# Moving four key projections and one set of values from between the attention layers into them

## The chip, the cores and the metric

The kernel runs on one core of a Trainium2 chip. The core has five engines that run their own instruction queues in order and meet only through semaphores: TensorE (PE, matrix products into the accumulator memory PSUM, with its weight loads shown as PEld), VectorE (DVE), ScalarE (ACT), GpSimd (POOL) and SyncE (SP, which issues the DMA transfers). The metric is the device time of one execution in microseconds; lower is better.

## The reference

Four layers act on one sequence of S = 2048 rows of D = 512 numbers: a sliding-block layer (A), a full layer (B), and both again. Each normalises its rows, projects them to queries, keys and values of 32 heads of 16 numbers, takes a softmax of scaled scores, sums the values with it, projects the result and adds it to the rows. Cut to what matters:

```python
x = x + _A_ref(_layernorm(x), A_wqkv, A_wo)     # row i sees rows i-255 .. i
x = x + _B_ref(_layernorm(x), B_wqkv, B_wo)     # every row sees every row
x = x + _A_ref(_layernorm(x), A_wqkv, A_wo)
x = x + _B_ref(_layernorm(x), B_wqkv, B_wo)

# inside both:
q, k, v = split_heads(x @ wqkv)
p = softmax(mask(q @ k.T * 16 ** -0.5))          # the mask only in A
out = merge_heads(p @ v) @ wo
```

## The kernel before

**Numbers.** Activations and weights are split into a high and a low float16 part, and a product is the sum of three products of parts (`TERMS`). A projection of 512 rows to 512 columns is therefore four tiles of 128 columns, each twelve products (four blocks of the inner dimension, three terms). One such product is a *piece*; the planner counts it as `MM` = 0.222 us. Twelve pieces end up in one PSUM bank or bank pair, `b`. Values are also made in half widths (`halves`): a piece is then half as long.

**Layers and chunks.** Layers are numbered 0 to 3; 0 and 2 slide, 1 and 3 are full. The rows are cut into NQ = 4 chunks of 512 (`c`). Heads are handled four at a time (`qd`, 8 of them); a column tile `ht` (or `t`, 0 to 3) of a projection holds eight heads, so it serves two `qd`. In the full layers one pass over all keys for one chunk and one `qd` is a *visit* of NT = 16 steps. In each step, for two pairs of heads, PE makes scores (L764), ACT takes their exponential (`e`, L772, 128x1024 numbers at a time), and PE multiplies an earlier step's exponentials with the values (L821) into `acc`. Layer 1 goes chunk by chunk (visits 0 to 7 are chunk 0, 8 to 15 chunk 1, ...). Layer 3 goes column tile by column tile, in 16 groups of two visits.

**Side work.** Everything else, the projections for the same layer and for the next, norms, transposes and output projections, is cut into pieces and put between the attention's steps by a planner that runs when the kernel is built. It fixes the order of PE's instructions (and in the full layers DVE's) with a clock of its own, `clock[0]`. A `Work` is a generator with a cost, a name, the names that it depends on, and, with `w`, a weight tile that must have been loaded (it becomes ready 8 us of the planner's clock after the load; ring 0 has two such tiles). A `Side` holds a list of works for a stretch of steps. In a sliding layer `step` runs works up to a share of the whole cost. In a full layer it calls `share`, after the second scores of every step but a visit's first, with one more call in the visit's second step, so that a visit has sixteen calls. `share` adds to `budget` the cost still left divided by the steps still left (at least `least`), caps it at 0.75 us, and runs pieces of the first work in the list that is ready, until about two full pieces have run, the budget is used up, or `b` isn't free. After the twelfth piece `b` counts as taken for another 2 us (`PH["free"]`), while DVE joins its two halves, so that a call is lost there.

**Squares and shifts.** After a key or query projection the sums of squares of its rows are needed (`sq`, on ACT or POOL; summed on PE by `hsum`, L556 or L559). This last part (`rest`) is put on the list `pend`, due 4.6 us later in a full layer, and `settle` carries it out, in `share` only when `b` isn't in use; `b` then counts as taken for 2 us again. For queries it gives the row maxima `m`, which are written to `qs` (L603). For keys it gives maxima in `KM`, and with the last chunk of a column tile `key_shift` makes the tile's shift from all four chunks, writes it to `kf` (L624) and notes `("S", l, ht)` as done. The keys of a full layer lie in DRAM as `kf`, the queries as `qs`; `kt` and `qt` are the tiles loaded from them for a visit (L795, L786).

**When a visit may start.** `attention` loads `kt` and `qt` of the next visit as soon as neither `lacking` (the key and query projections that it needs) nor `owing` (their shift or maxima) holds. If a visit begins and that hasn't happened, it forces side work out:

```python
            if not win and not ahead:
                while lacking(c, qd) or owing(c, qd):
                    if lacking(c, qd) or PH["busy"]:
                        sd.one(True)
                    else:
                        settle()
                ahead.append(load_full(l, c, qd))
```

**Which work goes where.** Layer 0's works (`side0`) hold the key projections K(1,0), K(1,1) and K(1,2) of layer 1, four column tiles each, beside its own. Its tail (`tails[0]`), which runs without attention, ends with layer 1's transposes T(1,3) and the last chunk's keys for tiles 0 and 1 (K1(0), K1(1)). Layer 1 has two Sides: one for the first four visits, `works[1][0]`, which `finish` empties by force at its end, and one for the rest of the layer, `works[1][1]` (`side1()`), with 14 full projections. The tail of layer 2 (`tails[2]`) has values of layer 3 (VV(3,...)), the output projection OO(2,3), transposes T(3,3) and the keys K3(3,0). Layer 3's sixteen Sides come from `side3(t, c)`; at a group's end all but output projections (`O3`, which have no name) must be finished.

Of the kernel before, what the change touches and what calls it, by code (L numbers as in the profile page):

```python
# [35 lines left out]
RINGS = WB, VB  # L36
L_MIN = 2.0 ** -90
# [153 lines left out]
def fast_path(ctx, tc, flag, a_x, a_wqkv, a_wo, b_wqkv, b_wo, out):  # L191
# [298 lines left out]

    def project(l, s, c, act, ht=None, ring=0):


        ty, n = l % 2, f"{l}_{s}_{c}" + ("" if ht is None else f"_h{ht}")
        w = weights(ty, s, n, *((0, D, 0) if ht is None else (ht * P, (ht + 1) * P, ring)))
# [9 lines left out]
        for t in range(NHT) if ht is None else (ht,):  # L505
            ps = bank()
            w0 = t * P if ht is None else 0
# [54 lines left out]
    def quarters(ht):  # L562

        return slice(0, P) if ht is None else slice(32 * ht, 32 * ht + 32)

    def keys(l, c, act, ht=None, then=None, ring=0):
        sqs = yield from project(l, 1, c, act, ht, ring)

        def rest():
            ph = squares(f"k{l}_{c}_{ht}", sqs)  # L570
            if l not in KM:
                KM[l] = vp.tile([P, NQ], F32, name=f"km{l}", tag="km", bufs=2)
            r = quarters(ht)
            with tc.high_priority(HEAD_START):
                nc.vector.tensor_reduce(KM[l][r, c:c + 1], ph[r], axis=AX.XY if PH["full"] else AX.X, op=ALU.max)  # L575
                if then is not None:
                    then(l, ht)
        pend.append((clock[0] + (4.6 if PH["full"] else 3.6 if PH["win"] else 1.2), rest, (l, c, ht)))
# [347 lines left out]
    class Side:  # L926

        def __init__(self, steps, works=(), following=(), least=0.0):
            self.next, self.least = list(following), least
            self.q, self.steps, self.cost, self.spent, self.k = [], steps, 0.0, 0.0, 0  # L930
            self.budget = self.lag = 0.0
            for w in sorted(carried + list(works), key=lambda w: PH.get("full") and w.name is None):
                self.add(w)
            carried.clear()
# [56 lines left out]

        def share(self):

            self.budget = min(self.budget + max((self.cost - self.spent) / max(self.steps - 3 - self.k, 1), self.least), 0.75)
            self.lag = max(self.lag - 0.42, -0.3)
            if pend and not PH["busy"] and clock[0] >= max(PH["free"], pend[0][0], vt_[0] - 0.2):
                settle(False)
                PH["free"] = clock[0] + 2.0
                self.lag += 0.1
            s0 = self.spent  # L1000
            while (self.q and clock[0] >= PH["free"] and self.budget >= MM / 2 and (self.lag < 0.25 or self.budget > 0.45)
                   and self.spent - s0 < 1.5 * MM):
# [6 lines left out]
        def finish(self, keep=False):  # L1009

            stays = lambda w: (w.name is None and keep) if w.name is None else w.name[0] == "P"
# [17 lines left out]
    def attention(l, works):  # L1029
# [18 lines left out]
        for (g, c, qd), after in zip(visits, visits[1:]):  # L1048
# [27 lines left out]
            for f in (attn_win if win else attn_full)(l, c, qd, *ops, a):  # L1076
                drain()
                if f is None:
                    flush(1)
# [35 lines left out]
    def K(l, c, act=True):  # L1115
        return Work(later(keys, l, c, act), PK, ("K", l, c), [("T", l, c), ("P", l % 2, 1), ("P", l % 2, 0)], True)
# [12 lines left out]
    def K1(ht, act=False):  # L1129
        return Work(later(keys, 1, NQ - 1, act, ht, key_shift, act), PK / 4, ("K1", ht), [("T", 1, NQ - 1), ("P", 1, 1)], True, ring=act)  # L1130
# [108 lines left out]
    def side1():  # L1239
        m = [(ty, s) for ty in range(2) for s in range(4)]  # L1240
        a = [CW(*x, [("C", *y)] if y else [("Q", 1, 1)]) for y, x in zip([None] + m, m)]
        a += [Q(1, c, False) for c in (1, 2, 3)]
        for c in range(3):
            a += [OO(1, c), T(2, c)] + ([Q(2, c - 1, False)] if c else []) + [K(2, c, False), VV(2, c, False)]
        return a

    def side3(t, c):
# [6 lines left out]
        if t < 2 and (t or c > 1):  # L1254
            a.append(upper(3, 2 * t + c // 2, range(2 * (c % 2), 2 * (c % 2) + 2)))
        if (t, c) != (0, 0):
# [3 lines left out]
    works = [[side0(c) for c in range(NQ)], [[last_lower(1), K1(2), upper(1, 2), upper(1, 3), K1(3)], side1()], [side2(c) for c in range(NQ)],  # L1260
# [3 lines left out]
             2: [VV(3, 0, True, (0,)), OO(2, 3, True), VV(3, 1, True, (0,), late(3)), VV(3, 2, True, (0,), late(3)), VV(3, 0, True, (1,), late(3)), T(3, 3), K3(3, 0, True, True)]}  # L1264
# [54 lines left out]
```

## Time and profile before

| | us |
|---|---|
| median of three runs | 2701.3 |
| the runs | 2702.79, 2701.3, 2694.14 |
| profiled execution | 2691.39 |
| its span, first to last instruction | 2689.5 |
| first scores of layer 1 | 447.45 |
| first scores of layer 3 | 1706.87 |

In the span, PE is busy 92% and ACT 88%. The granted clock of TensorE averages 0.993 of full speed. Times in timelines are counted from the start of the span. A row of a timeline has the start, the time, the engine, the line, the operation, output and inputs with buffer numbers left out, and the number of instructions merged into the row; in brackets stands how long the engine was idle before it and what it waited for. A matmul's shown time contains its way through the array, some 0.2 us, in which the next one already runs, so merged rows of PE overlap by that much. In the chain of waits a row has its start, its time, and the engine and line, or the DMA, on which the end depended at that moment.

### The profile page before, as it was taken

How to read it: one execution, taken by the hardware profiler on the slowest of the kernel's cores; microseconds unless marked ns; L12 is line 12 of the kernel's file. 1: busy time of each engine (PE TensorE's matmuls, PEld its weight loads, DVE VectorE, ACT ScalarE, POOL GpSimd, SP SyncE). 2: the span in 40 equal slices, each digit the busy share in tenths (PEclk: the TensorE clock that was granted, in tenths of full speed). 3: DMA queues.
4: the chain of work that ended last, by engine and by line, in shares of the span. 5: the costliest groups of instructions: out<-in, count | busy, mean ns of one | idle time of the engine just before them, and what ended most of it. 6: DMA issues, size and time to landing. Idle time of an engine off the chain costs nothing.

```text
span 2689.5 us, 120844 instructions
## 1 busy us (share of the span) xinstructions
PE 2470.9 (92%) x54767; PEld 1135.1 (42%) x54767; DVE 1107.3 (41%) x2350; ACT 2363.7 (88%) x2671; POOL 529.4 (20%) x1072
## 2 busy tenths in 40 slices
PE   7889999999998999999999999899999999998996
PEld 3334454444443444444444444534444443433332
DVE  5576453223334334334336666233333333333333
ACT  4666765999999999999996776799999999999996
POOL 1556550001000100100116886000000000000000
PEclk9999999999999999999999999999999999999998
DMA  8898875232334325324227655423333323333332
GB/s 277 248 287 266 237 200 156 67 97 89 107 94 125 96 86 151 100 87 114 93 82 209 193 166 163 133 83 112 93 94 101 101 88 113 101 107 121 122 120 96
DMA packets 341189, 361.29 MB, mean 134 GB/s; under 512 B 117800, under 2 KB 256568, under 8 KB 334392
## 3 DMA queue, kind: packets, MB, share of 16 engines
q1 hardware_dynamic: 340664, 353.46, 44.1%
q8 instruction: 430, 7.05, 1.1%
q14 instruction: 95, 0.78, 0.1%
HBM read 240.65 MB, written 96.99 MB: 126 GB/s over the span
## 4 chain that ended last, share of the span: by engine, by line
ACT 56%; PE 24%; issue 11%; DVE 5%; DMA 3%; POOL 0%; SPq 0%; ACTq 0%; DVEq 0%; POOLq 0%
ACT e L772 55%; PE b L406 8%; PE acc L854 4%; PE acc L821 3%; PE s L768 2%; PE s L764 2%; PE bs L409 2%; PE b L409 2%; PE b L402 1%; DVE xh L461 0%; DMA x<-in_A_x_dram 0%; DVE xn L455 0%; DVE xh L455 0%; DVE ot L731 0%; DMA qt<-qs 0%
## 5 line engine op out<-in xcount | busy, mean ns | idle before, releaser
L772 ACT ACTIVATE e<-s 128x1024 f32<-128x1024 f32 (+2 forms) x2432 | 2241.6, 1056 | 140.8 <-PE s L768 107.9
L821 PE MATMUL acc<-e,vt 64*17 64x512 f32 x16384 | 1092.0, 590 | 0.8 <-issue 0.8
L764 PE MATMUL s<-qt,kt 64*32 64x512 f16 x16384 | 855.6, 381 | 125.1 <-ACT e L772 100.2
L764 PEld LDWEIGHTS <-kt 64*32 64x32 f16 x16384 | 407.6, 89 | 934.9 <-issue 854.5
L821 PEld LDWEIGHTS acc<-e,vt 64*17 64x17 f32 x16384 | 282.9, 92 | 65.8 <-issue 6.9
L847 POOL TENSOR_SCALAR_AFFINE_SELECT e<-e 128x256 f32<-128x256 f32 x512 | 229.6, 455 | 154.5 <-ACT e L772 153.6
L844 POOL TENSOR_SCALAR_AFFINE_SELECT e<-e 128x256 f32<-128x256 f32 x448 | 199.4, 451 | 97.7 <-ACT e L772 96.3
L854 PE MATMUL acc<-e,vt 128*17 128x384 f32 (+2 forms) x2816 | 202.5, 389 | 2.2 <-POOL e L844 1.9
L749 POOL TENSOR_TENSOR oh<-o,oh 128x512 f16<-128x512 f32 x31 | 36.1, 1164 | 720.5 <-DVE oh L748 716.9
L428 DVE TENSOR_SCALAR sa<-acc 128x512 f32<-128x512 f32 x64 | 44.3, 691 | 287.7 <-PE acc L821 287.7
L406 PE MATMUL b<-xc,w 128*32 128x512 f16 x2496 | 151.7, 387 | 11.2 <-DVE km L575 6.7
L714 DVE SCALAR_TENSOR_TENSOR x<-b,x 128x512 f32<-128x512 f32 x122 | 83.8, 687 | 183.4 <-PE b L402 180.1
L534 POOL TENSOR_TENSOR sq_h<-sp_h 128x512 bf16<-128x512 f16 x29 | 43.1, 1485 | 556.9 <-DVE sp_h L528 556.9
L768 PE MATMUL s<-qt,kt 64*128 64x384 f16 (+2 forms) x1408 | 120.9, 276 | 27.4 <-ACT e L772 21.1
L534 POOL TENSOR_TENSOR sq<-sp 128x512 bf16<-128x512 f16 x32 | 45.7, 1432 | 504.3 <-DVE sp L528 481.1
L402 PE MATMUL b<-xc,w 64*32 64x512 f16 x3072 | 127.2, 376 | 1.5 <-DVE j L429 0.8
L428 DVE TENSOR_SCALAR vt<-b 128x256 f32<-128x256 f32 (+1 forms) x36 | 18.4, 512 | 236.0 <-PE b L402 222.9
L402 PE MATMUL b<-wo,oh 64*32 64x512 f16 x2592 | 108.8, 376 | 6.4 <-DVE x L714 3.8
L402 PE MATMUL b<-xc,w_h 64*32 64x512 f16 x2784 | 110.6, 376 | 0.0
L406 PEld LDWEIGHTS <-w 128*32 128x32 f16 x2496 | 76.5, 99 | 74.8 <-issue 24.9
L428 DVE TENSOR_SCALAR j_h<-b 128x512 f32<-128x512 f32 x29 | 20.0, 690 | 213.2 <-PE b L402 213.2
L428 DVE TENSOR_SCALAR j<-b 128x512 f32<-128x512 f32 x32 | 22.0, 688 | 202.3 <-PE b L402 202.3
(142 smaller groups left out, 1971.6 us busy)
## 6 DMA issues: line engine op xcount, KB each, us to landing
kt<-kf SPq DMA_DIRECT2D x128, 512.0 KB
qt<-qs SPq DMA_DIRECT2D x128, 256.0 KB
xd<-x SPq DMA_DIRECT2D x96, 256.0 KB
x<-xd SPq DMA_DIRECT2D x96, 256.0 KB
w<-wd SPq DMA_DIRECT2D x21, 1024.0 KB
kt<-kw SPq DMA_DIRECT2D x64, 256.0 KB
qs<-sp SPq DMA_DIRECT2D x48, 256.0 KB
wo<-wd SPq DMA_DIRECT2D x12, 1024.0 KB
```

The lines of the kernel that those rows point to most:

```text
L402: nc.tensor.matmul(ps[g:g + 32, r], a[k, g:g + 32], b[k], start=(i == 0), stop=(i == len(pairs) - 1), skip_group_check=True)
L406: nc.tensor.matmul(ps[g:g + 32], a[:, g:g + 32], b, start=(i == 0), stop=(i == len(pairs) - 1), skip_group_check=True)
L409: nc.tensor.matmul(ps, a, b, start=(i == 0), stop=(i == len(pairs) - 1))
L428: nc.vector.tensor_scalar(dst, ps[0], scale, None, op0=ALU.mult)
L534: nc.gpsimd.tensor_tensor(sq, sp[:, 0], sp[:, 0], ALU.mult)
L764: nc.tensor.matmul(ps[g:g + 32, h], kt[R * h:R * h + R, pr, kc + g:kc + g + 32], qt[R * h:R * h + R, pr], start=True, stop=True, skip_grou ...
L768: nc.tensor.matmul(ps[:, h, s0:s0 + wd_], kt[R * h:R * h + R, pr, kc:kc + P], qt[R * h:R * h + R, pr, qc:qc + wd_], start=True, stop=True)
L772: nc.scalar.activation(e[:, :, w0:w1], ps[:, :, w0:w1], AF.Exp, scale=SCALE)
L821: nc.tensor.matmul(acc[r][32 * h:32 * h + DH + 1, :], V[l, qd // 4, j // 8][k, j % 8, 4 * (qd % 4) + h, :], es_[h // 2][k, h % 2, :], star ...
L844: nc.gpsimd.affine_select(v, v, pattern=[[0, 2], [-1, P]], compare_op=ALU.is_gt, fill=0.0, base=0, channel_multiplier=1)
L847: nc.gpsimd.affine_select(v, v, pattern=[[0, 2], [1, P]], compare_op=ALU.is_ge, fill=0.0, base=0, channel_multiplier=-1)
L854: nc.tensor.matmul(a[32 * h:32 * h + DH + 1, q * P:(q + nb) * P], V[l, (4 * c + j) // 4][:, j % 4, 4 * qd + h, :], es_[h // 2][:, h % 2, s ...
```

## The change

Keys of layer 1: `LATER_K` names, for each column tile, the chunks whose projection leaves layer 0: chunk 2 for tile 2, chunks 0, 1 and 2 for tile 3. K(1,0) and K(1,1) then make three tiles, K(1,2) two, and the four quarters are made in layer 1 as `K1c(c, ht)`. K1(ht), with the shift, now waits for them. The first Side of layer 1 gets K1c(2,2), K1c(0,3) and K1c(1,3) and gives K1(3) up; the second begins with K1c(2,3) and K1(3). What belongs to tile 3 may be carried over from the first to the second (`finish`). In `side1`, the queries Q(1,2) and Q(1,3) move from the front to behind OO(1,0) and OO(1,1).

Values of layer 3: VV(3, 0, (1,)), the upper half-width values of chunk 0, leaves the tail of layer 2; `side3` makes them in the first two groups of layer 3, two tiles each.

The planner: `share` may run four half pieces in a call instead of three or four. It notes in `missed` that `b` wasn't free, and `extra` then runs one piece in the next step, between the first scores and the values, if no settle is due.

```diff
+LATER_K = (), (), (2,), (0, 1, 2)
...
+    def tiles_of(ht):
+        return range(NHT) if ht is None else ht if type(ht) is tuple else (ht,)
...
     def project(l, s, c, act, ht=None, ring=0):
-        w = weights(ty, s, n, *((0, D, 0) if ht is None else (ht * P, (ht + 1) * P, ring)))
+        ts = tiles_of(ht)
+        w = weights(ty, s, n, *((0, D, 0) if ht is None else (ts[0] * P, (ts[-1] + 1) * P, ring)))
...
-        for t in range(NHT) if ht is None else (ht,):
+        for t in ts:
             ps = bank()
-            w0 = t * P if ht is None else 0
+            w0 = (t - ts[0]) * P
...
     def quarters(ht):
-        return slice(0, P) if ht is None else slice(32 * ht, 32 * ht + 32)
+        ts = tiles_of(ht)
+        return slice(32 * ts[0], 32 * ts[-1] + 32)
...
+        def extra(self):
+            if self.missed and self.q and not (pend and pend[0][0] <= clock[0] + 1.8) and self.budget >= MM / 2 and clock[0] >= PH["free"] - 0.45 and not PH["busy"]:
+                c = self.one()
+                if c is not None:
+                    self.budget -= abs(c)
+                    self.lag += abs(c)
+            self.missed = False
...
         def share(self):
...
+            self.missed = clock[0] < PH["free"]
...
-                   and self.spent - s0 < 1.5 * MM):
+                   and self.spent - s0 < 1.9 * MM):
...
         def finish(self, keep=False):
-            stays = lambda w: (w.name is None and keep) if w.name is None else w.name[0] == "P"
+            stays = lambda w: (w.name is None and keep) if w.name is None else w.name[0] == "P" or w.name[:2] == ("K1", 3)
...
                 if f is None:
+                    if not win and u > 2:
+                        sd.extra()
                     flush(1)
...
     def K(l, c, act=True):
-        return Work(later(keys, l, c, act), PK, ("K", l, c), [("T", l, c), ("P", l % 2, 1), ("P", l % 2, 0)], True)
+        ts = tuple(t for t in range(NHT) if c not in LATER_K[t]) if l == 1 else None
+        return Work(later(keys, l, c, act, ts), PK * len(tiles_of(ts)) / NHT, ("K", l, c), [("T", l, c), ("P", l % 2, 1), ("P", l % 2, 0)], True)
...
     def K1(ht, act=False):
-        return Work(later(keys, 1, NQ - 1, act, ht, key_shift, act), PK / 4, ("K1", ht), [("T", 1, NQ - 1), ("P", 1, 1)], True, ring=act)
+        return Work(later(keys, 1, NQ - 1, act, ht, key_shift, act), PK / 4, ("K1", ht),
+                    [("T", 1, NQ - 1), ("P", 1, 1)] + [("K1", ht, c) for c in LATER_K[ht]], True, ring=act)
+
+    def K1c(c, ht):
+        return Work(later(keys, 1, c, False, ht), PK / 4, ("K1", ht, c), [("T", 1, c), ("P", 1, 1)], True)
...
     def side1():
-        a += [Q(1, c, False) for c in (1, 2, 3)]
+        a += [Q(1, 1, False)]
         for c in range(3):
-            a += [OO(1, c), T(2, c)] + ([Q(2, c - 1, False)] if c else []) + [K(2, c, False), VV(2, c, False)]
+            a += [OO(1, c), T(2, c)] + ([Q(1, c + 2, False)] if c < 2 else []) + ([Q(2, c - 1, False)] if c else []) + [K(2, c, False), VV(2, c, False)]
...
     def side3(t, c):
-        if t < 2 and (t or c > 1):
+        if t < 2:
             a.append(upper(3, 2 * t + c // 2, range(2 * (c % 2), 2 * (c % 2) + 2)))
...
-    works = [[side0(c) for c in range(NQ)], [[last_lower(1), K1(2), upper(1, 2), upper(1, 3), K1(3)], side1()], [side2(c) for c in range(NQ)],
+    works = [[side0(c) for c in range(NQ)], [[last_lower(1), *[K1c(c, 2) for c in LATER_K[2]], K1(2), upper(1, 2), upper(1, 3), K1c(0, 3), K1c(1, 3)],
+                                                   [K1c(2, 3), K1(3)] + side1()], [side2(c) for c in range(NQ)],
              [side3(t, c) for t in range(NHT) for c in range(NQ)]]
...
-             2: [VV(3, 0, True, (0,)), OO(2, 3, True), VV(3, 1, True, (0,), late(3)), VV(3, 2, True, (0,), late(3)), VV(3, 0, True, (1,), late(3)), T(3, 3), K3(3, 0, True, True)]}
+             2: [VV(3, 0, True, (0,)), OO(2, 3, True), VV(3, 1, True, (0,), late(3)), VV(3, 2, True, (0,), late(3)), T(3, 3), K3(3, 0, True, True)]}
```

More of the change, by code (lines that the diff above doesn't have):

```diff
@@ L489, in transpose @@
             transposed(l, c, i, xh)
+    def tiles_of(ht):
+        return range(NHT) if ht is None else ht if type(ht) is tuple else (ht,)
     def project(l, s, c, act, ht=None, ring=0):
-        ty, n = l % 2, f"{l}_{s}_{c}" + ("" if ht is None else f"_h{ht}")
-        w = weights(ty, s, n, *((0, D, 0) if ht is None else (ht * P, (ht + 1) * P, ring)))
+        ty, n = l % 2, f"{l}_{s}_{c}" + ("" if ht is None else f"_h{tiles_of(ht)[-1]}")
+        ts = tiles_of(ht)
+        w = weights(ty, s, n, *((0, D, 0) if ht is None else (ts[0] * P, (ts[-1] + 1) * P, ring)))
         yield wait(8)
@@ L569, in rest @@
         def rest():
-            ph = squares(f"k{l}_{c}_{ht}", sqs)
+            ph = squares(f"k{l}_{c}_{tiles_of(ht)[-1]}", sqs)
             if l not in KM:
@@ L930, in __init__ @@
             self.q, self.steps, self.cost, self.spent, self.k = [], steps, 0.0, 0.0, 0
-            self.budget = self.lag = 0.0
+            self.budget, self.lag, self.missed = 0.0, 0.0, False
             for w in sorted(carried + list(works), key=lambda w: PH.get("full") and w.name is None):
```

## The prediction

> **What bounds the kernel now.** I read the page first, then busy time by stage, then the timeline and the chain of waits at the places that the change touches.
>
> ```profile
> PE 2470.9 (92%) x54767; PEld 1135.1 (42%) x54767; DVE 1107.3 (41%) x2350; ACT 2363.7 (88%) x2671; POOL 529.4 (20%) x1072
> ```
>
> ```profile
> 311.00:405.90 94.90, 91.21 (x1636) 45.97 (x1632) 49.18 (x119) 65.99 (x83) 56.60 (x142) 1.00 0.69 202
> ```
>
> ```profile
> 684.00:1399.40 715.40, 676.82 (x16976) 305.57 (x16961) 276.80 (x545) 709.40 (x770) 52.19 (x41) 1.00 0.35 102
> ```
>
> The columns of a stage are its length, then busy PE, PEld, DVE, ACT and POOL, the granted clock, the DMA share and GB/s. The page's totals hide two regimes. In the last third of layer 0 (311 to 406 us) PE is busy 96% and ACT 70%: PE time taken out there is time saved. In layer 1 ACT is busy 99% and PE 95%: PE work put there is free as long as it never makes ACT wait. The change moves work from the scarce place to the covered one, so the question is whether layer 1 has room at the moment when the results are due.
>
> One step of layer 1, and the forced end of its first four visits:
>
> ```profile
> 560.33 0.63 PE L402 MATMUL b<-xc,w_h 64*32 64x512 f16 x16
> 560.88 0.41 PE L764 MATMUL s<-qt,kt 64*32 64x512 f16 x8
> 561.09 1.05 PE L821 MATMUL acc<-e,vt 64*17 64x512 f32 x16
> 561.95 0.41 PE L764 MATMUL s<-qt,kt 64*32 64x512 f16 x8
> 562.16 0.63 PE L402 MATMUL b<-xc,w_h 64*32 64x512 f16 x16
> ...
> 565.83 1.49 PE L402 MATMUL b<-xc,w_h 64*32 64x512 f16 x48
> ```
>
> ```profile
> 567.66 5.00 ACT L772 ACTIVATE e<-s 128x1024 f32<-128x1024 f32 x5 [0.42 <-PE s L764]
> ```
>
> A step lasts 1.83 us (560.33 to 562.16): 0.2 us of score, 0.86 of values, 0.2 of score, then at most two side pieces of 0.22 (x16 is two pieces); some 0.1 us is spare. Sixteen steps are a visit. The x48 is side work forced out at step 64: ACT then idles 0.42 before 567.66. So after the last scores of a step (565.83) ACT has work for 567.66 - 0.42 - 565.83 = 1.41 us.
>
> **The change, part by part.**
>
> *Layer 0 loses four quarter projections.*
>
> ```profile
> 297.87 2.59 PE b L406 x48
> ```
>
> ```profile
> 387.25 3.64 PE L406 MATMUL b<-xc,w 128*32 128x512 f16 x64
> ...
> 397.21 3.64 PE L406 MATMUL b<-xc,w 128*32 128x512 f16 x64
> ```
>
> The chain of waits runs through PE here: side work like this row, then scores and values, then side work again. A quarter is 48 matmuls, 2.59 us. One each leaves K(1,0) and K(1,1), two leave K(1,2), whose 192 matmuls are three rows of x64 (the first and the last shown): 4 x 2.59 = **-10.4**. Bounds: K(1,2) starts only when its transposed rows are there, and half of its share may be lost to that wait (-7.8); the ACT copies and `kf` writes that leave, with DMA at a share of 0.69, could add a little (-11).
>
> *First four visits.* They lose K1(3) and gain K1c(2,2), K1c(0,3) and K1c(1,3). The forced end goes, since third quarters (`ht` 3) may now be carried on: **-0.4**. Late instead is what was carried; that is the part on visit 6.
>
> *Room.* Four quarters are 4 x 2.66 us of PE (twelve pieces of 0.22) in a layer where it idles 5% (39 of 715 us in its larger part). Their joins on DVE (busy 277 of 715 us), their squares on POOL (52) and two `kf` writes and a weight load each on SP lie beside that: nothing. The higher limit lets four half-width pieces run in a step; 4 x 0.11 is what two full ones take. `extra` puts 0.22 of PE into the step after one that had no side piece. It stalls only where the copy out of `b` is late; bounds 0 and +2, and I take 0.
>
> *When the third quarters are due.* This decides the sign.
>
> ```profile
> 497.65 0.63 PE L402 MATMUL b<-wv,xc 64*32 64x256 f16 x32
> ...
> 504.98 0.52 PE L402 MATMUL b<-wv,xc 64*32 64x256 f16 x24
> ```
>
> ```profile
> 576.15 0.38 PE L556 MATMUL b<-sq_h,hsum 64*32 64x512 bf16 x2
> ...
> 578.40 0.29 SPq L624 DMA_DIRECT2D kf<-mk  x1
> ...
> 579.78 0.63 PE L402 MATMUL b<-xc,w 64*32 64x512 f16 x16
> ```
>
> Twelve pieces fill `b`, then a step is lost while DVE empties it. A half-width tile at four pieces a step takes 4 steps (497.65 to the next tile at 504.98 is 4 x 1.83; x32 is four pieces), a quarter 7. Settling a quarter's squares (L556) costs two more steps and happens only between groups. Counted by these rules the first 64 steps hold: last_lower in 3 to 10, K1c(2,2) and K1(2) with their two settles to 27, eight upper tiles of 4 steps to 59 (a visit's boundary, which hides a lost step, helps once), and 10 of K1c(0,3)'s 12 pieces. From step 64 on, 2 + 3 x 12 = 38 pieces are left up to the end of K1(3). The new Side paces 732 pieces (14 works of 48 and four quarters, with 0.3 us added to each projection) over 445 steps, 1.64 a step: 38 / 1.64 = 23 steps. The lost steps and the settles between them bring K1(3)'s end to about step 91. Its shift `S` waits until its squares are settled, and by then Q(1,1)'s first group has begun in `b`. But visit 6 begins at step 96, and there `owing` forces that group and the settle out before `kt` may be loaded. The scores that wait stand ahead of the last two steps' values in PE's order, so PE stops as well as ACT.
>
> ```profile
> 2174.22 0.29 SPq L624 DMA_DIRECT2D kf<-mk  x1
> 2176.11 0.91 SPq L795 DMA_DIRECT2D kt<-kf  x2
> ```
>
> ```profile
> 551.42 0.36 SPq L795 DMA_DIRECT2D kt<-kf  x1
> ```
>
> ```profile
> 554.40:555.40 1.00, 0.98 (x48) 0.57 (x39) 0.00 (x0) 1.00 (x3) 0.00 (x0) 1.00 0.22 66
> ```
>
> The price: square sum to `kf` write 2.25 (576.15 to 578.40), write to load 1.89 (2174.22 to 2176.11), load 3.2 (issued at 551.42; a DMA share of 0.22 in the last microsecond puts its end near 554.6), score and ACT's start 0.5 (0.41 at 560.88, and a handover): 7.8, less ACT's 1.41, +6.4. If Q(1,1)'s group is in `b`, 6 to 8 pieces and the emptying of `b` (two DVE passes, 1.6) come first, up to +9.8. And PE then idles some 4 us or more:
>
> ```profile
> 449.70:453.10 3.40, 2.82 (x40) 0.79 (x47) 0.00 (x0) 2.99 (x4) 0.00 (x0) 0.51 1.00 281
> ```
>
> ```profile
> 453.62 113.62 ACT L772 ACTIVATE e<-s 128x1024 f32<-128x1024 f32 x123 [0.93 <-PE s L764]
> ```
>
> After PE's pause at the start of layer 1 the granted clock was 0.51 for 3.4 us, and ACT waited 0.93. So the stall is 6.4 to 10.7; I take **+8.5**, the middle. [...]
>
> *Q(1,1) for chunk 1.*
>
> ```profile
> 653.30 0.41 PE L556 MATMUL b<-sq,hsum 64*32 64x512 bf16 x8
> ...
> 655.30 1.30 SPq L603 DMA_DIRECT2D qs<-m_None  x4
> ```
>
> ```profile
> 2186.71 1.31 DMA qs<-m
> ...
> 2188.09 2.62 DMA qt<-qs
> ```
>
> Q(1,1) started at 579.78, step 72, and its row maxima were settled at 653.30, step 112; they are due at 128. Now it starts near 95, behind three quarters. Four groups of about 7.3 steps, the first partly forced, end near 118; Q(1,2)'s first group, its weights long there, comes next, and the settle falls on step 127. The chain: 2.0 to the `qs` writes (653.30 to 655.30), about 2.3 for four of them (issued in 1.30, each landing in 1.31), 2.62 for `qt`, 0.5 to ACT: 7.4, against 1.83 + 1.41 of cover, **+4.2**. Two steps earlier it costs 0.5; not settled by the boundary, 9.4 (8 forced pieces 1.8, emptying 1.6, chain 7.4, less 1.41).
>
> *End of layer 1.* The last chunk's side work becomes ready only with that chunk and is the same as before, so what is forced out at the end stays: 0, with one group of twelve pieces as bounds, -2.7 and +2.7.
>
> *Tail of layer 2.*
>
> ```profile
> 57.22 3.19 DMA xc<-xh
> ```
>
> ```profile
> 1689.86 5.34 SPq L483 DMA_TRANSPOSE xc<-xh  x3
> ```
>
> ```profile
> 1694.11 1.48 PE b L409 x12
> ...
> 1699.52 2.59 PE b L409 x12
> ```
>
> The removed values are four tiles, 5.2 us of PE (1694.11 to about 1699.4), but they cover the transposes, which are issued until 1695.2 and land 3.2 later: K3(3,0) could start at 1698.4 instead of 1699.4. The weight load that leaves SP's queue ahead of them gives 0.5 at most. **-1.2**, bounds 0 and -2; a gain of 5.2 isn't to be had.
>
> *Layer 3* makes these values in its first two groups, which then hold 48 pieces in 32 steps as later ones do. The first has no output projection that it may carry on, and by my step rules wants some 37 steps, so about 2 us are forced at its end, where ACT's 1.41 and half a step of PE cover part: **+1.3**, bounds 0 and 2.2.
>
> Sum: -10.4 - 0.4 + 8.5 + 4.2 - 1.2 + 1.3 = **+2.0 us**. The profiled execution took 2691.39 (span 2689.5), so 2693.4. The median of the runs shown is 9.9 above it; on that scale the forecast is 2701.3 + 2.0 = **2703.3**.
>
> **The rivals.**
>
> *No stall (faster).* If `S` is settled by step 92 and Q(1,1) by 124, both stalls go: -10.7, 2690.6. For it: without the pacing, 38 pieces and the lost steps need only some 26 steps from 64, and `extra` begins groups earlier. Against it: a settle that misses one gap between groups waits for a whole further group, 7 steps. Chance 0.26.
>
> *Visit 8 misses its boundary (slower).* One more lost step in 32 puts Q(1,1)'s settle past step 128. Then Q(1,2)'s open group is forced first, 9.4 in place of 4.2, and with the open group at visit 6 too (10.7): -10.7 + 10.7 + 9.4 = +9.4, 2710.7. For it: next to a boundary the settle at 576.15 came 5.6 steps after the group's end. Chance 0.16.
>
> *Layer 0 gives back half.* Taking matmuls from K(1,2) does nothing if the wait for its rows ends last: 5.2 more, 2708.5. Against it: the three x64 rows follow each other with only scores and values between. Chance 0.06.
>
> **How the numbers follow.** The forecast has 0.52; alone it spans 2697 to 2709 (visit 6 from 6.4 to 10.7, visit 8 from 0.5 to 9.4). 0.3% is 8 us, about what a measurement can tell from no change. Faster: four fifths of the first rival and a little of the forecast's lower end, 0.24. Slower: over half of the second rival, part of the third, a little of the forecast's upper end, 0.16. Within: 0.60. The range, 2687 to 2712, takes in the first rival with 3.6 us for its unknown costs and the second.
>
> **What would show it.** Layer 0 ends some 10 us earlier, and layer 1's scores start near 437. ACT shows a gap of 6 to 11 us about 176 us later (visit 6), with PE waiting for `kt<-kf`, and one of up to 10 at 234 us (visit 8), for `qt<-qs`. No gaps there: the first rival. K3(3,0) waits on the transposes. I am wrong if PE in layer 0 finds new waits, or if layer 1's gaps stand elsewhere.

## The result, and the profile after

The changed kernel takes **2715.78 us**, the median of five runs (2710.99 to 2720.5); the kernel before takes 2698.35 in five (2694.14 to 2702.79). The ratio is **1.0063**, with a 95% interval of 1.0048 to 1.0079: slower by 17 us, where 2 us were forecast and 2712 was the range's upper end. The profiled execution took 2720.5 (span 2718.8).

The page of the kernel after, its busy times:

```profile
PE 2478.5 (91%) x55299; PEld 1135.1 (42%) x55299; DVE 1126.9 (41%) x2374; ACT 2365.1 (87%) x2659; POOL 539.2 (20%) x1076
```

PE's busy time is 7.6 us more than before and ACT's 1.4 us more, in a span that is 29.3 us longer. So the loss is waiting. (The profiled executions are not the medians: that of the kernel after is the slowest of its five, that of the kernel before took less than each of its five. So single profiles show more than the 17 us.) Where it lies is told by the start of ACT's first exponential in each layer (the runs of the experiments stand in the same table, which the later sections use; "layer 3" ends with the start of its last exponential). One of e5's six executions took 7782.52 us, in a slow state, and isn't in its ratio.

| kernel | ratio to before, 95% | layer 1 starts at | layer 1 | layer 2 | layer 3 |
|---|---|---|---|---|---|
| before | 1 | 448.0 | 956.3 | 303.1 | 958.2 |
| after | 1.0063 [1.0048, 1.0079] | 441.9 | 980.6 | 306.4 | 968.5 |
| e1 no extra | 1.0008 [0.9999, 1.0017] | 436.4 | 973.9 | 303.5 | 958.5 |
| e2 three quarters | 1.0019 [1.0010, 1.0028] | 439.1 | 964.3 | 303.6 | 968.7 |
| e3 values in the tail | 1.0057 [1.0043, 1.0071] | 433.3 | 980.5 | 305.6 | 964.4 |
| e4 extra alone | 1.0024 [1.0012, 1.0035] | 447.6 | 956.3 | 304.2 | 967.8 |
| e5 three, no extra | 0.9947 [0.9934, 0.9960] | 438.5 | 957.7 | 306.8 | 957.2 |
| e6 e5, values in the tail | 0.9948 [0.9935, 0.9962] | 438.6 | 956.6 | 302.8 | 958.5 |
| e7 e6 with two quarters | 0.9942 [0.9930, 0.9954] | 447.4 | 951.3 | 302.8 | 955.3 |
| e8 limit alone | 0.9995 [0.9985, 1.0005] | 451.7 | 957.9 | 303.4 | 959.6 |
| e9 e7 with no quarter | 0.9966 [0.9954, 0.9977] | 451.9 | 950.9 | 303.2 | 959.0 |
| e10 third piece | 0.9979 [0.9968, 0.9990] | 447.4 | 958.8 | 302.1 | 956.6 |
| e11 e7 and third piece | 0.9937 [0.9921, 0.9952] | 444.4 | 952.8 | 304.6 | 959.4 |
| e12 e11 with four quarters | 1.0018 [1.0008, 1.0028] | 436.6 | 976.2 | 307.3 | 957.4 |

In the kernel after, layer 1 starts 6.1 us earlier, then takes 24.3 longer, layer 2 takes 3.3 longer and layer 3 10.3. In layer 2, e1 and e2 have the same work and show 303.5 and 303.6, e5 306.8: single profiles spread by as much as the 3.3. (The line numbers of the kernel after are seven higher for scores, L771, exponentials, L779, and values, L828; side products are at L403 and L410, square sums at L562 and L565, the loads of `kt` and `qt` at L802 and L793, the writes from `mk` and `m` at L631 and L610.)

**Visit 6.** The timeline of the kernel after, all engines:

```profile
613.45 0.38 PE L562 MATMUL b<-sq_h,hsum 64*32 64x512 bf16 x2
...
615.16 0.39 PE L562 MATMUL b<-sq_h,hsum 64*32 64x512 bf16 x2 [1.33 <-DVE km L582]
...
615.87 7.60 ACT L779 ACTIVATE e<-s 128x1024 f32<-128x1024 f32 x8 [1.03 <-PE s L771]
...
622.05 1.93 PE L403 MATMUL b<-xc,w 64*32 64x512 f16 x64
624.04 0.69 DVE L429 TENSOR_SCALAR j<-b 128x512 f32<-128x512 f32 x1 [7.22 <-PE b L403]
...
625.51 0.39 PE L562 MATMUL b<-sq_h,hsum 64*32 64x512 bf16 x2 [1.54 <-DVE j L430]
625.55 0.43 DVE L534 CAST sp<-j 128x512 f16<-128x512 f32 x1
...
626.01 0.69 DVE L535 TENSOR_TENSOR sp<-j,sp 128x512 f16<-128x512 f32 x1
...
626.73 1.23 DVE L582 TENSOR_REDUCE km<-b 32x1 f32<-32x1024 f32 x1
...
628.57 0.29 SPq L631 DMA_DIRECT2D kf<-mk  x1
630.39 1.39 SPq L802 DMA_DIRECT2D kt<-kf  x3
...
634.52 0.63 PE L771 MATMUL s<-qt,kt 64*32 64x512 f16 x8 [8.62 <-DMA kt<-kf]
...
635.28 1.02 ACT L779 ACTIVATE e<-s 128x1024 f32<-128x1024 f32 x1 [11.82 <-PE s L771]
```

Read it downwards. Two quarters' square sums are settled together; the second waits 1.33 for DVE and stands ahead of scores, so ACT loses 1.03. At the visit's end x64, eight pieces of Q(1,1)'s open group, are forced out, `b` is emptied, the last square sum made, the shift written, `kt` loaded, and only then scores are made: ACT idles **11.82**. Two more gaps follow while PE is slow, 1.11 and 0.40, so the place costs 14.4. The windows of the same kernel around it (columns as in the prediction):

```profile
628.00:634.50 6.50, 0.00 (x0) 0.00 (x0) 0.50 (x2) 0.00 (x0) 0.00 (x0) 0.50 0.53 150
634.50:638.50 4.00, 3.98 (x56) 1.21 (x64) 0.00 (x0) 2.05 (x2) 0.00 (x0) 0.58 0.48 184
```

**Visit 8.** First the chain of waits of the kernel after, then ACT's timeline:

```profile
693.07 0.34 PE b L562 x8
...
694.87 0.29 SPq L610
...
696.27 0.39 SPq L802
...
696.76 5.12 DMA qt<-qs
```

```profile
702.77 1.02 ACT L779 ACTIVATE e<-s 128x1024 f32<-128x1024 f32 x1 [6.65 <-PE s L771]
704.90 1.02 ACT L779 ACTIVATE e<-s 128x1024 f32<-128x1024 f32 x1 [1.11 <-PE s L771]
706.71 1.94 ACT L779 ACTIVATE e<-s 128x1024 f32<-128x1024 f32 x2 [0.78 <-PE s L771]
```

Q(1,1)'s square sums are made in the visit's last step but one (step 126, counted from 0), so one step and ACT's 1.41 cover the chain, as forecast. But behind the four writes to `qs` another `kt` load goes first, and `qt` then takes 5.12. ACT loses 6.65 + 1.11 + 0.78 = 8.5.

The two stalls make 22.9 us in layer 1, which is 24.3 longer. What else happens there nearly cancels: by the table `extra` costs 6.7 (e1), and without quarters and without `extra` the other edits take 5.4 off (e9); together that makes 24.2. The 10.3 us of layer 3 have no such place; the experiments show what they are.

### The profile page after: what moved, and what is told of

It reads as the page before. It is cut to its first block, busy times and chain, and to the rows that moved or that the text cites. A ratio compares the mean times of both kernels' runs of the same rounds, so it can differ in the third digit from the quotient of the medians.

```text
span 2718.8 us, 121915 instructions
## 1 busy us (share of the span) xinstructions
PE 2478.5 (91%) x55299; PEld 1135.1 (42%) x55299; DVE 1126.9 (41%) x2374; ACT 2365.1 (87%) x2659; POOL 539.2 (20%) x1076
## 4 chain that ended last, share of the span: by engine, by line
ACT 55%; PE 25%; issue 12%; DVE 5%; DMA 2%; SPq 0%; POOL 0%; ACTq 0%; DVEq 0%
ACT e L779 54%; PE b L407 8%; PE acc L861 4%; PE acc L828 3%; PE s L775 2%; PE s L771 2%; PE bs L410 1%; PE b L410 1%; PE b L403 1%; DMA kt<-kw 1%; DMA xc<-xh 1%; DVE xh L462 1%; DVE xn L456 0%; DVE xh L456 0%; DVE ot L738 0%
## 5 line engine op out<-in xcount | busy, mean ns | idle before, releaser
L779 ACT ACTIVATE e<-s 128x1024 f32<-128x1024 f32 (+2 forms) x2432 | 2249.7, 1047 | 167.6 <-PE s L775 103.6
L828 PE MATMUL acc<-e,vt 64*17 64x512 f32 x16384 | 1093.1, 592 | 0.7 <-issue 0.7
L771 PE MATMUL s<-qt,kt 64*32 64x512 f16 x16384 | 854.9, 381 | 140.5 <-ACT e L779 101.2
L771 PEld LDWEIGHTS <-kt 64*32 64x32 f16 x16384 | 403.7, 89 | 930.7 <-issue 839.0
L828 PEld LDWEIGHTS acc<-e,vt 64*17 64x17 f32 x16384 | 281.5, 93 | 73.4 <-issue 5.2
L854 POOL TENSOR_SCALAR_AFFINE_SELECT e<-e 128x256 f32<-128x256 f32 x512 | 232.6, 462 | 146.9 <-ACT e L779 145.8
L851 POOL TENSOR_SCALAR_AFFINE_SELECT e<-e 128x256 f32<-128x256 f32 x448 | 202.1, 458 | 95.6 <-ACT e L779 92.8
L540 POOL TENSOR_TENSOR sq_h<-sp_h 128x512 bf16<-128x512 f16 x33 | 48.6, 1474 | 577.1 <-DVE sp_h L534 577.1
L407 PE MATMUL b<-xc,w 128*32 128x512 f16 x1920 | 120.4, 394 | 11.2 <-DVE km L582 6.7
L403 PE MATMUL b<-xc,w_h 64*32 64x512 f16 x3168 | 128.9, 376 | 0.8 <-DVE j_h L430 0.8
L403 PE MATMUL b<-xc,w 64*32 64x512 f16 x3072 | 126.5, 376 | 0.9 <-DVE j L430 0.8
L403 PE MATMUL b<-wo,oh 64*32 64x512 f16 x2592 | 111.3, 376 | 3.0 <-DVE x L721 2.3
L403 PE MATMUL b<-wv,xc 64*32 64x256 f16 (+1 forms) x3840 | 105.1, 304 | 4.7 <-DVE m L598 3.4
L775 PEld LDWEIGHTS <-kt 64*128 64x128 f16 x1408 | 52.8, 95 | 128.8 <-issue 109.1
```

The costliest lines, as they stand in the source:

```text
L403: nc.tensor.matmul(ps[g:g + 32, r], a[k, g:g + 32], b[k], start=(i == 0), stop=(i == len(pairs) - 1), skip_group_check=True)
L407: nc.tensor.matmul(ps[g:g + 32], a[:, g:g + 32], b, start=(i == 0), stop=(i == len(pairs) - 1), skip_group_check=True)
L540: nc.gpsimd.tensor_tensor(sq, sp[:, 0], sp[:, 0], ALU.mult)
L771: nc.tensor.matmul(ps[g:g + 32, h], kt[R * h:R * h + R, pr, kc + g:kc + g + 32], qt[R * h:R * h + R, pr], start=True, stop=True, skip_grou ...
L775: nc.tensor.matmul(ps[:, h, s0:s0 + wd_], kt[R * h:R * h + R, pr, kc:kc + P], qt[R * h:R * h + R, pr, qc:qc + wd_], start=True, stop=True)
L779: nc.scalar.activation(e[:, :, w0:w1], ps[:, :, w0:w1], AF.Exp, scale=SCALE)
```

## The experiments

Each ratio is to the kernel before on the same chip. 0.001 is 2.7 us. "By the plan" means by the planner's own clock, which fixes the order of the instructions when the kernel is built.

**e1, the changed kernel without `extra`.**

```diff
                 if f is None:
-                    if not win and u > 2:
-                        sd.extra()
                     flush(1)
```

> The changed kernel without the extra pieces between scores and values; all else as changed. The changed kernel stands at 1.0063 of the kernel before, some 17 us. Theory 'extra costs': by the planner's rules extra puts 57 pieces into layer 1 and 80 into layer 3; in the trace 30 + 36 of ACT's long pitches, 8.6 + 11.7 us together, stand beside one. A part of that is work that goes elsewhere, so about 12 us come back: ratio 1.002 (1.000 to 1.004). Theory 'stalls alone': extra costs nothing, the loss is the two stalls of visits 6 and 8, which stay: 1.006 within 0.001. Third: extra spares work that is otherwise forced out at ends; without it slower, over 1.007.

Measured: 1.0008, so `extra` costs 0.0055, some **14.8 us** within the change (the two intervals don't touch). Layer 3 returns to 958.5, layer 1 gets 6.7 shorter. Both stalls stay, as ACT's timeline of e1 shows:

```profile
629.47 1.02 ACT L779 ACTIVATE e<-s 128x1024 f32<-128x1024 f32 x1 [11.71 <-PE s L771]
...
696.30 1.02 ACT L779 ACTIVATE e<-s 128x1024 f32<-128x1024 f32 x1 [6.06 <-PE s L771]
```

**e4, `extra` alone in the kernel before** (the method `extra` itself, as in the change, isn't shown again).

```diff
             self.lag = max(self.lag - 0.42, -0.3)
+            self.missed = clock[0] < PH["free"]
...
                 if f is None:
+                    if not win and u > 2:
+                        sd.extra()
                     flush(1)
```

> The kernel before with the extra pieces alone added (missed noted in share, one piece between first scores and values); no quarter moved, limit 1.5 kept. Theory 'extra costs': the same cost as in the changed kernel, 8 to 16 us: ratio 1.0045 (1.003 to 1.006). Theory 'stalls alone': 1.000 within 0.001. Third: the forced ends shrink (21 forced pieces' steps in layer 1's plan in place of 54), faster by 2 to 4 us: 0.999.

Measured: 1.0024, 6.5 us slower, below the 1.003 to 1.006 expected. Layer 3 is 9.6 us longer than before, as in the changed kernel. Layer 1 isn't: there `extra` also shortens what is forced out at the layer's end (from the last exponential of layer 1 to the first of layer 2 it is 4.9 us before and 2.6 in e4). So it does behind layer 3 (from its last exponential to the span's end 24.0 before, 21.4 in e4). In the changed kernel the first is 2.6 and the second 21.3 to 21.4, with and without `extra`, so these 4.9 us aren't set against its cost there. The rest of what lies between 6.5 and 14.8 isn't explained.

What it costs at one place, in PE's timeline of e4 (layer 3):

```profile
2266.25 0.41 PE L764 MATMUL s<-qt,kt 64*32 64x512 f16 x8 [0.51 <-ACT e L772]
2266.47 0.41 PE L402 MATMUL b<-wo,oh 64*32 64x512 f16 x8
2266.68 1.05 PE L821 MATMUL acc<-e,vt 64*17 64x512 f32 x16
2267.54 0.41 PE L764 MATMUL s<-qt,kt 64*32 64x512 f16 x8
2267.76 0.63 PE L402 MATMUL b<-wo,oh 64*32 64x512 f16 x16
2268.19 0.41 PE L764 MATMUL s<-qt,kt 64*32 64x512 f16 x8
...
2269.26 0.41 PE L764 MATMUL s<-qt,kt 64*32 64x512 f16 x8
2270.07 0.41 PE L764 MATMUL s<-qt,kt 64*32 64x512 f16 x8 [0.39 <-ACT e L772]
```

The step before had no side piece, yet its idle time can't be used: the first scores (2266.25) must wait for ACT to free their buffer. From there to the second scores a step without it takes 1.07 (2268.19 to 2269.26); with the extra piece (2266.47) it takes 1.29. ACT, which begins an exponential every 0.92, is then ready before these scores are: by the start times in the trace it begins one at 2266.99 and the next at 2268.08, 1.09 later, and 0.17 is lost. The two steps take 3.82, not 3.66. A second way to lose stands at visits' ends. There a group that is ahead by an extra piece can fill `b` at a worse moment (this is argued from one place, not tested); all engines of e4:

```profile
2258.63 0.69 DVE L428 TENSOR_SCALAR sa<-acc 128x512 f32<-128x512 f32 x1 [10.47 <-PE acc L821]
...
2260.79 1.38 DVE L714 SCALAR_TENSOR_TENSOR x<-b,x 128x512 f32<-128x512 f32 x2
...
2262.22 0.63 PE L402 MATMUL b<-wo,oh 64*32 64x512 f16 x16 [0.76 <-DVE x L714]
...
2263.19 1.02 ACT L772 ACTIVATE e<-s 128x1024 f32<-128x1024 f32 x1 [0.54 <-PE s L764]
```

DVE empties `acc` first, so `b` comes free late, PE's next side piece waits 0.76 and ACT 0.54. The same step of the kernel before has no such gap.

**e10, the same pieces at another place.** The kernel before, with three pieces in `share` in the step after one that had none.

```diff
+            late, self.missed = self.missed, clock[0] < PH["free"]
...
-                   and self.spent - s0 < 1.5 * MM):
+                   and self.spent - s0 < (1.5 + late) * MM):
```

> The kernel before with up to three pieces, in place of two, in the step after one that had none, at the usual place behind the second scores. By the plan this happens in 60 steps of layer 1 and 72 of layer 3, about as often as extra did (61 and 80), which cost 0.0024. Theory 'the place costs': extra delays the second scores by 0.22 us in a step whose first scores had just waited for ACT, and each such step comes out 0.17 us long; behind the second scores there is room, so nothing is lost: 1.000 (0.9985 to 1.0005). Rival 'the amount costs': 0.22 us more of PE in a step that has 0.1 to spare costs the same wherever it stands: 1.0024 (1.0015 to 1.0035).

Measured: 0.9979 [0.9968, 0.9990], 5.7 us **faster**, where `extra` lost 6.5 with about as many pieces. PE's timeline of e10:

```profile
2275.03 0.41 PE L764 MATMUL s<-qt,kt 64*32 64x512 f16 x8 [0.35 <-ACT e L772]
2275.24 1.05 PE L821 MATMUL acc<-e,vt 64*17 64x512 f32 x16
2276.10 0.41 PE L764 MATMUL s<-qt,kt 64*32 64x512 f16 x8
2276.31 0.84 PE L402 MATMUL b<-xc,w_h 64*32 64x512 f16 x24
2276.96 0.41 PE L764 MATMUL s<-qt,kt 64*32 64x512 f16 x8
...
2278.69 0.41 PE L764 MATMUL s<-qt,kt 64*32 64x512 f16 x8
```

The second scores come 1.07 after the first, as always. The three pieces make this step 1.93 long and the next 1.73: PE has made up the 0.1 by then. ACT still loses a little: by the start times one exponential comes 1.01 after the one before it, in place of 0.92. Taken over all such steps in the middle of visits, from one exponential to the second after it, a step with an extra piece takes 2.05 in layer 1 and 2.01 in layer 3 of e4 (medians of 23 and 29), where others take 1.83; the step behind one with three pieces takes 1.94 in both layers of e10 (medians of 35 and 47). The few steps that follow take 1.81, so some 0.06 of either delay is made up. So both count, the place and the amount, but the place more: a piece between the scores costs ACT an estimated 0.12 to 0.15 us, one behind them 0.04. That e10 even gains on the whole I hadn't expected. In the profile layer 3 is 1.6 us shorter than before and the stretch from the last exponential to the span's end 2.4 (24.0 to 21.6), while layer 1 is 2.5 longer; which of these makes the gain, one profile doesn't settle.

**e2, three quarters.** K(1,1) is whole in layer 0 again.

```diff
-LATER_K = (), (), (2,), (0, 1, 2)
+LATER_K = (), (), (2,), (0, 2)
...
-... upper(1, 3), K1c(0, 3), K1c(1, 3)],
-    [K1c(2, 3), K1(3)] + side1()], ...
+... upper(1, 3), K1c(0, 3), K1c(2, 3)],
+    [K1(3)] + side1()], ...
```

> The changed kernel with three quarters moved, not four: K(1,1) is made whole in layer 0 again (+2.6 us there), K1c(2,3) takes the place of K1c(1,3) in the first Side, and the second begins with K1(3). By the planner's rules K1(3)'s shift is then settled at step 91 with nothing forced at visit 6, and Q(1,1)'s maxima at step 122 in place of 126. Theory 'stalls': the gaps of ACT at visit 6 (14.4 us with its small ones) and visit 8 (8.5 us) go, 22 less 2.6 comes back: ratio 0.999 (0.997 to 1.001), extra still in. Rival 'slack': a good part of these gaps only took the place of waits that come anyway, about half comes back: 1.003. Rival 'stalls move': the load of kt is issued some 4 steps after the settle and is late all the same: 1.005 or more.

Measured: 1.0019, 12 us better than the changed kernel. Layer 1 is 16.3 shorter (980.6 to 964.3). That is less than the first theory's 19 and more than the second's 9; whether a part of the stalls is left is seen without `extra`, in e5.

**e5, three quarters and no `extra`** (the edits of e1 and e2).

> The changed kernel without extra and with three quarters moved (K(1,1) whole in layer 0). The two mends gave 1.0063 to 1.0008 and 1.0063 to 1.0019 by themselves. Theory 'two separate costs': they add up, ratio 1.0063 - 0.0055 - 0.0044 = 0.9964 (0.995 to 0.9975), faster than the kernel before by the layer 0 saving of 2.6 us a quarter and 2 us more of forced ends that the higher limit spares; ACT shows no gap over 2 us in layer 1. Rival 'same cost twice': without extra the steps run on time so that the stalls were already cheaper, or the other way round; 0.999 or above.

Measured: **0.9947**, a little beyond the sum of the two (0.9964, expected down to 0.995). ACT's timeline of e5 from visit 5 into visit 8:

```profile
613.35 7.60 ACT L779 ACTIVATE e<-s 128x1024 f32<-128x1024 f32 x8 [1.04 <-PE s L771]
621.23 74.15 ACT L779 ACTIVATE e<-s 128x1024 f32<-128x1024 f32 x80 [0.28 <-PE s L771]
```

The double settle's 1.04 is still there; the load of `kt` is late by 0.28 only, and visit 8 begins without a gap. So both stalls hang on due times that one quarter less meets.

**e3, the values back in layer 2's tail.**

```diff
-        if t < 2:
+        if t < 2 and (t or c > 1):
             a.append(upper(3, 2 * t + c // 2, range(2 * (c % 2), 2 * (c % 2) + 2)))
...
-... VV(3, 2, True, (0,), late(3)), T(3, 3), ...
+... VV(3, 2, True, (0,), late(3)), VV(3, 0, True, (1,), late(3)), T(3, 3), ...
```

> The changed kernel with the upper values of chunk 0 of layer 3 back in the tail of layer 2 (and out of layer 3's first two groups). Theory 'the pause halves the clock': without them PE idles 5.84 us ahead of K3's keys and then makes these at half clock (5.10 us a tile, not 2.6); with them PE has no such pause, the way from the tail's output projection to layer 3's first scores goes from 28.9 back to 27.6, and layer 3 loses 5.2 us of PE work and a half-clock window at its start: 3 to 6 us come back, ratio 1.0045 (1.004 to 1.0055). Rival 'values hidden in layer 3': the move is worth what was meant, a few us are lost by undoing it: 1.007 to 1.008. Rival 'neither': 1.006.

**e6, the same on e5.**

> As the one before, with the upper values of chunk 0 of layer 3 also back in the tail of layer 2. Theory 'the pause halves the clock': the tail is then 1.3 us shorter, and layer 3 has 5.2 us less of side work in its first two groups and a shorter half-clock window at its start: 2 to 4 us faster than the one before, about 0.9953. Rival 'neither' (as the run with extra, 1.0057 beside 1.0063, can't exclude): 0.9964. Rival 'values hidden': 0.997 to 0.998.

Measured: 1.0057 beside 1.0063, and 0.9948 beside 0.9947. That is 'neither': the move of the values is worth nothing that these intervals (some 4 us to each side) can tell. The pause is real, though. PE's timelines of the tail, first the kernel after, then e6:

```profile
1711.17 1.47 PE L410 MATMUL bs<-wv,xc 128*128 128x256 f16 x12
1718.48 5.10 PE L410 MATMUL b<-xc,w_h 128*128 128x512 f16 x12 [5.84 <-DMA xc<-xh]
```

```profile
1684.67 1.48 PE L410 MATMUL bs<-wv,xc 128*128 128x256 f16 x12 [1.71 <-DMA wv<-wd]
...
1689.92 2.75 PE L410 MATMUL bs<-xc,w_h 128*128 128x512 f16 x12
```

Without the values the keys K3 start earlier but take 5.10 in place of 2.75 (granted clock 0.51 in 1718.40:1723.40 of the kernel after). From the last tile of the output projection to layer 3's first scores it is 28.9, 26.6, 26.9 and 26.7 us in four profiles without the values (after, e1, e2, e5), and 27.6, 28.8, 27.7 and 28.1 in four with them (before, e3, e6, e7). About 0.7 us is gained there and given back in layer 3's first two visits (62.1 us on average in those four, 61.1 in these).

**e7, two quarters** (on e6: `LATER_K = (), (), (2,), (2,)`, so K1c(2,2) and K1c(2,3)).

> As the one before with two quarters moved, K1c(2,2) and K1c(2,3), so that K(1,0) and K(1,1) are both whole in layer 0. K1(3)'s shift is settled at step 86 by the plan, in place of 91, and Q(1,1)'s maxima at 120 in place of 123. Theory 'layer 0 pays by the quarter': slower than the one before by 2.6 us, 0.001. Rival 'three is still late': at step 91 the load of kt lands at step 95 to 96 at the earliest, so some of visit 6's stall remains with three quarters and not with two: the same as the one before or 1 to 3 us faster.

Measured: 0.9942, the same as e6 within the intervals. Layer 0 gives 8.8 us back in the profile, layer 1 wins 5.3. ACT's timeline of e7 from the end of visit 4 into visit 8:

```profile
591.43 115.45 ACT L779 ACTIVATE e<-s 128x1024 f32<-128x1024 f32 x125
```

125 exponentials without a gap that the timeline shows. So the double settle's gap goes too, but the expected reason, a late `kt`, was no more than 0.28 us with three.

**e9, no quarter** (on e7: `LATER_K` empty, the second Side begins with K1(3)), and **e8**, the kernel before with the limit of 1.9 alone.

> The version with two quarters moved, but now with none: K(1,0), K(1,1) and K(1,2) whole in layer 0; the higher limit, the later place of Q(1,2) and Q(1,3), K1(3) at the head of the second Side and the values in layer 2's tail stay, no extra. With two quarters it was 0.9942. Theory 'quarters pay': each is worth 2.6 us of layer 0, so 0.9961 (0.9955 to 0.997). Rival 'the order pays': the gain is from layer 1's and layer 3's ends, where less is forced out, and the quarters are worth nothing: 0.9942 within 0.001. The limit alone gave 0.9995 and so isn't the whole of it.

> The kernel before with the limit of 1.9 pieces in share in place of 1.5, nothing else. By the plan the forced end of layer 1's first Side (five pieces) and two of layer 3's group ends (ten each) vanish. Theory 'forced ends cost ACT': 0.4 us for the first and 1 to 2 for each of the others, 2 to 4 us faster, 0.999. Rival 'four half pieces crowd the step': 0.44 us of side work where 0.33 stood adds waits of 0.1 to 0.2 us in some 60 steps that have it; 1.001 or more.

Measured: e9 0.9966, e8 0.9995. The limit alone gives nothing that can be measured, which decides for neither expectation of e8. Two quarters are worth 0.0024 (the intervals just touch), 6.5 us, near the first theory's 5.2. The rest of e7's gain, 0.0034, is there without any quarter. Layer 1 is 5.4 us shorter than before in e9, of which 2.1 are the end of the layer (4.9 to 2.8); what the later Q(1,2) and Q(1,3) and the later K1(3) each give was not parted.

**e11, two quarters and the third piece** (e7 with the edit of e10, the limit being `1.9 + late`).

> The version with two quarters moved, no extra and the values in layer 2's tail (0.9942), with the third piece behind the second scores added. Theory 'the place costs': Q(1,1)'s maxima settle at step 119 in place of 120 and less is forced out at layer 1's end; no loss, 0 to 2 us gained: 0.9938 (0.993 to 0.9945). Rival 'the amount costs': 6 us lost, 0.9965.

Measured: **0.9937** [0.9921, 0.9952], the fastest of all, though not told apart from e7. Again the third piece costs nothing on the whole.

**e12, all four quarters with the third piece and no `extra`** (e11 with the `LATER_K` of the change).

> The changed kernel with all four quarters moved, no extra, the values back in layer 2's tail, and the third piece behind the second scores. With two quarters this was 0.9937. By the plan K1(3)'s shift is still not settled at step 96, where four pieces (in place of seven) and the settle are forced, and Q(1,1)'s maxima settle at step 126 as before. Theory 'the due times decide': two quarters more save 5 to 6.5 us in layer 0, but visits 6 and 8 stall again by 11 to 14 and 5 to 8 us: 11 to 16 us slower than with two quarters, 0.9985 (0.997 to 1.0005). Rival 'the stalls were the late steps': with the steps in time the stalls shrink to a few us and four quarters win: 0.993 or below.

Measured: 1.0018, 0.0081 above e11; more than expected. ACT's timeline of e12:

```profile
629.67 1.02 ACT L779 ACTIVATE e<-s 128x1024 f32<-128x1024 f32 x1 [10.96 <-PE s L771]
...
697.03 1.02 ACT L779 ACTIVATE e<-s 128x1024 f32<-128x1024 f32 x1 [6.04 <-PE s L771]
```

With the small gaps beside them they make 14.0 and 8.3 us. Four forced pieces in place of eight make little odds: the chain behind them is the same.

## Why the prediction was wrong

**The step that failed is `extra`, taken at 0 with bounds 0 and +2.** It costs 14.8 us within the change (e1). I reasoned that it stalls only where the copy out of `b` is late, that is, by the amount of work in a step. That case exists (the 0.54 gap of e4), but most of the cost comes from where the piece stands: between first scores that waited for ACT and second scores that ACT soon needs. There a step takes 2.01 to 2.05 us in place of 1.83 (e4). The rows of one step stood in the prediction; the spare 0.1 us that I read there was a step's whole, not that stretch's. About as many pieces behind the second scores (e10) delay ACT by half of that, most of which is made up, and lose nothing on the whole.

**The stalls were right in place and cause and too small in size.** Both came where the prediction put them, a step or two earlier than it counted: K1(3)'s last piece in step 89 (91 was counted), Q(1,1)'s first in step 93 (95), a group and a settle forced out ahead of step 96, Q(1,1)'s square sums in step 126 (127). (The steps 72 and 112 that it read in the kernel before are 70 and 110 when counted from 0; the sum doesn't use them.) I took 8.5 for the first where it measured 14.4. My own count said that Q(1,1)'s group would be open in `b`, which was the upper branch; I took the middle of both. The rest is in the rows: the eight forced pieces and the emptying of `b` took the 3.4 of that branch (622.05 to 625.51), but Q(1,1)'s casts (0.43 and 0.69) stand before the maximum in DVE's order, so square sum to write took 3.06 and not 2.25; of three loads issued together the one that was waited for took 4.1 (630.39 to 634.52), not 3.2; the half clock, which I had carried over from the start of layer 1 as an estimate, came here too (0.50 and 0.58 in the windows above) and cost 1.51, not 0.9; and the double settle's 1.03 wasn't counted. For the second I took 4.2, and it measured 8.5: `qt` landed 5.12 after its issue, not 2.62, and the half clock's 1.89 was left out (0.54 in 702.00:706.50). The load wasn't alone: the DMA engines moved 327 GB/s, at a share of 1.05, in the last 3 us before the scores; the windows of the kernel after:

```profile
699.00:702.00 3.00, 0.00 (x0) 0.02 (x1) 0.00 (x0) 0.00 (x0) 0.00 (x0) 0.55 1.05 327
```

The row that I took the 2.62 from wasn't alone either, but there the `kt` load was issued 0.92 behind `qt`:

```profile
2188.09 0.87 SPq L786 DMA_DIRECT2D qt<-qs  x2
2189.01 0.48 SPq L795 DMA_DIRECT2D kt<-kf  x1
```

In the kernel after it goes 0.49 ahead of `qt`. That the order and the traffic make the difference is likely; no run here parts them.

**Layer 0** was right. Over all profiles layer 1 starts at 449.3 on average with no quarter moved (five: before, e4, e8, e9, e10) and at 437.0 with four (after, e1, e3, e12): 12.3, where 10.4 was forecast. Single profiles spread by 8.6 us there, and that of the kernel after shows 6.1. So the rival by which layer 0 gives back half fell. That each quarter brings its 2.6 isn't shown: the averages are 449.3 with none, 445.9 with two (e7, e11), 438.7 with three (e2, e5, e6) and 437.0 with four. The two tiles out of K(1,2) thus bring 3.4 where 5.2 were forecast, and the one out of K(1,0) 7.2 where 2.6 were; with that spread the split stays open. **The end of layer 1** won 2.3 (0 was forecast, with bounds of 2.7). **Layer 2's tail and layer 3's first group** came out at nothing together, as forecast (-1.2 and +1.3), but I didn't see the half clock (0.51 there).

**The rivals.** Without `extra` the sum of +2.0 was met, 1.0008 being 2.2 us, but by cancelling: the stalls were 10 us dearer, layer 0 and layer 1's end cheaper by 4, and the other edits gain more than I gave them (e9, 0.0034 with no quarter). "No stall" fell; no version with four quarters was without. "Visit 8 misses" named the right place, but its settle came in time; the load made it dear.

## What to carry to other kernels

When a step has time to spare, ask between which two instructions: a piece that fits into the step can still delay the one result for which the bottleneck engine waits, so side work goes behind the last instruction of the step that feeds that engine. When work is moved out of a scarce stage into a covered one, count its due time in steps with every settling and emptying, and price the miss as the whole chain (forced group, the queue of each engine in it, write, load beside other loads, and a slow PE after the pause, here half its clock for 3.3 to 4.8 us of work). Here two quarters met their due times and were worth having, three came out the same within the intervals, and four weren't worth it.

## What the runs showed of the hardware

In the profiles of before and after PE's granted clock went to 0.50 in stretches of 3.41, 6.83 or 10.24 us (449.75:453.16 before; 443.27:450.10 and 627.59:637.83 in the kernel after), once, twice or three times 3.41. (Only a profile's last stretch, cut by the span's end, is no such multiple: 9.64 and 7.67.) After the kernel after's pauses of 8.6, 7.1 and 5.8 us it was half until 3.3 to 4.8 us of work had passed (0.50 in 628.00:634.50, 0.58 in 634.50:638.50), and after 4.2 to 4.5 us K3's keys took 4.44 (e1, e2, e5). With the values in the tail, where PE paused up to 3.1 us ahead of these, the keys took 2.75. The length of a pause alone doesn't tell what follows it: in the kernel before PE paused 2.92 us, up to 60.54, and the clock was 0.50 in 60.63:64.04, while after a pause of 2.98 us, up to 130.11, it was 1.00 in 130.11:133.60. At the start of layer 1 PE waits 1.51 us in before and 1.52 in after, e1, e3, e7 and e9. Behind it the clock was 0.50 in 449.75:453.16 before and in 443.27:450.10 in the kernel after. The first sixteen products with the values took 1.95 in both, 1.96 in e1 and e3, 1.65 in e7 and 1.05 in e9. The kernel after loses 1.10 there, and 0.26 and 0.77 in the two gaps that follow; e9, after the same wait, nothing. ACT's timelines, after and e9:

```profile
447.65 1.02 ACT L779 ACTIVATE e<-s 128x1024 f32<-128x1024 f32 x1 [1.10 <-PE s L771]
```

```profile
451.87 6.52 ACT L779 ACTIVATE e<-s 128x1024 f32<-128x1024 f32 x7 [1.64 <-PE s L771]
```

Behind waits of the same length ACT thus lost 2.1 us and nothing. What decides isn't shown, as no run here moved a pause on purpose.
